# Placing each unit's value products directly ahead of the next unit's scores, and moving a tile's first unit, in a fused attention and two-layer feed-forward kernel

## The chip, the cores and the metric

The kernel runs on one core of a Trainium2 chip. The metric is the device time of one execution in microseconds (us); the time before is the median of three runs. One further execution was taken by the hardware profiler, and all rows below come from it.

## What is computed

Chunked attention with a few memory keys, then two feed-forward blocks. All in float32.

```python
# q, k, v: (4, 8, 768, 64); mem_k, mem_v: (4, 8, 8, 64)
for c in range(24):                                  # chunks of 32 positions
    q_c = q[:, :, 32*c : 32*c + 32]
    ctx = slice(max(0, 32*c - 16), min(768, 32*c + 40))
    k_full = concatenate([mem_k, k[:, :, ctx]], axis=2)
    v_full = concatenate([mem_v, v[:, :, ctx]], axis=2)
    out[chunk] = softmax(q_c @ k_full.T / 8) @ v_full
x  = out as (3072 tokens, 512)
h  = x @ w_in                                        # 512 -> 2048
x1 = softplus(h) @ w_out                             # 2048 -> 512
y  = ((x1 @ w_a) * (x1 @ w_b)) @ w_o2                # 512 -> 1536 -> 512
```

## The kernel before

The 3072 tokens are cut into 8 tiles of 384 (TT). For a tile, `emit_h` multiplies x by one block of 128 columns of w_in (12 products into one PSUM bank of tag "h", which has two banks), `emit_soft` makes softplus of it (three ScalarE activations that start from the bank, then a VectorE operation, line 558, that reads the bank for the last time, then a split into a high and a low part), and `emit_x1` multiplies by w_out two rounds later (LAG) into four "acc" banks. A tile has 16 such rounds f. Every product is done in three parts on split operands, which is why there are 12 matmuls where 4 would do. After the 8 tiles a last stage computes the second feed-forward block (lines 740 to 850); the change doesn't touch it.

The attention of tile t + 1 is computed between the products of tile t. Its work is cut into units of 128 queries of all 8 heads, three to a tile: units 3t + 3, 3t + 4 and 3t + 5 during tile t, called the first, middle and last unit of their tile here. In the code i is the unit's number less 3. Units 0 to 2 are computed ahead of everything, as blocks. Units 3 to 5 run during tile 0 with steps of their own (EARLY_STEPS). The steps of a unit are:

- load_v (SyncE): the values of the unit's two windows of 88 positions and the memory values, into the one set of value tiles vn (SETS = 1), which the products of the unit before must have read
- turn (VectorE): transposes of k and q into kt and qt (one buffer each), and two small ScalarE copies of the memory keys into kt
- scores (TensorE, line 430): 32 products of 64x64 weights with 96 columns into two banks of tag "att"
- soft, norm: softmax on VectorE, ScalarE and GpSimd
- flip, flip2 (VectorE): ten 32-row transposes of the weights into af (one buffer)
- values (TensorE, line 477): 32 products of 96x64 weights with 64 columns into one bank pxa of tag "att"; the first 16 use window 0 and the transposes of flip, the other 16 window 1 and those of flip2
- place: ScalarE and VectorE copy pxa into x of the next tile as a high and a low part (lines 484 and 485)

Where a step stands is fixed by hand. `plan` holds (time, unit, step); a time of 32t + s means slot s of tile t, and a slot is half a round: `att_at` is called after `emit_h` (even slots) and after `emit_x1` (odd slots) and issues all steps that are due. From the second tile to the last but one, TensorE, VectorE and SyncE execute in the order in which the program issues; ScalarE and GpSimd are ordered by the framework's scheduler.

`Loaded.fetch(t, part)` brings k and q of a whole tile into one buffer in four parts of eight DMAs (part 0 has up to four more for the edges of a sequence, and four on GpSimd's queue for the memory keys). It is issued during the tile before, after the turn of that tile's last unit, which must have read the buffer. The weights of the last stage are converted meanwhile by `Early` (fetch, top, value, store; five in a tile), whose DMAs are on the same SyncE queue.

The slots of a tile before, for units 9 and up: first unit: turn 30 and scores 32 counted from the tile before (thus 0 of the next), values 9, load of the next unit's values 10; middle unit: turn 9, scores 11, values 20, load 21; last unit: turn 19, fetch parts 20, 21, 22, 23, scores 21, values 30, load 31.

Of the kernel before, what the change touches and what calls it, by code (L numbers as in the profile page):

```python
# [9 lines left out]
F32 = mybir.dt.float32  # L10
# [12 lines left out]
         (3, "values"), (3.1, "place"))  # L23
START = 1.7
FIRST_STEPS = tuple((d + {"turn": 0.5, "flip": -1, "flip2": -1}.get(step, 0), step) for d, step in STEPS)
SETS = 1
EARLY_STEPS = (((4.9, "scores"), (5, "weigh"), (9, "flip_p"), (10.9, "values"), (11, "place")),
               ((12.9, "scores"), (13, "weigh"), (17, "flip_p"), (18.9, "values"), (19, "place")),
               ((21.9, "scores"), (22, "weigh"), (27, "flip_p"), (28.9, "values"), (29, "place")))
EARLY = len(EARLY_STEPS)  # L30
# [20 lines left out]
def attn_moe_moe2(ctx: ExitStack, tc: tile.TileContext, q, k, v, mem_k, mem_v,  # L51
# [7 lines left out]
    P = 128  # L59
# [6 lines left out]
    UPT = TT // QU  # L66
# [4 lines left out]
    KT = DM // P  # L71
# [6 lines left out]
        name=nc.get_next_instruction_name(), act_func_set_id=6, ins=[], outs=[]))  # L78
# [8 lines left out]
    ps = ctx.enter_context(tc.tile_pool(name="ps", bufs=2, space=PSUM))  # L87
# [18 lines left out]
    class Weight:  # L106


        def __init__(self, dst, key):
            self.dst, self.key = dst, key  # L110
# [114 lines left out]
    loaded = Loaded()  # L225
    vsets = [Values(i) for i in range(SETS)]

# [82 lines left out]
    class Block:  # L310
# [48 lines left out]
        def values(self):  # L359
            self.px = px = self.psum(4, "pxb")[:, :KT * QB].rearrange("p (i t) -> p i t", i=KT)  # L360
            for i in range(KT):
                for j in range(2):
                    r = slice(64 * j, 64 * j + 64)
                    nc.tensor.matmul(px[r, i], lhsT=self.vn[:, 2 * i + j, :], rhs=self.af[:, i, r], start=True, stop=True)
# [28 lines left out]
    class Unit:  # L393


        def __init__(self, u):
            self.u = u
            self.b, self.n = divmod(u, NU)

        def load_v(self):  # L400
            self.v = vsets[self.u % SETS]
            self.v.fetch(self.b, self.n)
# [66 lines left out]
        def values(self):  # L469
            u = self.u  # L470
            vn = self.v.v
            self.px = px = ps.tile([P, 512], F32, tag="att", name=f"pxa{u}").rearrange("p (i t) -> p i t", i=KT)

            for w in range(2):
                for i in range(KT):
                    for j in range(2):
                        nc.tensor.matmul(px[64 * j:64 * j + 64, i, QB * w:QB * w + QB], lhsT=vn[:, w, 2 * i + j],  # L477
                                         rhs=af[:, 2 * w:2 * w + 2, KT * j + i], start=True, stop=True)
# [18 lines left out]
    blocks = [Block(u) for u in range(BPT)]  # L497
    units = [Unit(u) for u in range(B * NU)]

    plan = []  # L500
    for i, unit in enumerate(units[UPT:]):
        at = 2 * NF1 * (i + 1) // UPT - START + NEXT_LATER * (i == EARLY) - (i % UPT == UPT - 1)
        steps = FIRST_STEPS if i % UPT == 0 else STEPS
        if i < EARLY:
            steps = EARLY_STEPS[i]
            at = steps[-1][0]
        plan += [(at + d - steps[-1][0], i, getattr(unit, step)) for d, step in steps]
        if i < SETS:
            plan.append((2 + i, -1, unit.load_v))
        if i + SETS < len(units[UPT:]):  # L510
            plan.append((at + 1, i, units[UPT + i + SETS].load_v))
        if i % UPT == UPT - 1 and unit.u + 1 < len(units):
            turned = at + steps[0][0] - steps[-1][0]
            plan += [(turned + 1 + part, i, partial(loaded.fetch, unit.u // UPT + 1, part)) for part in range(KT)]
    plan += [(at, -1, lambda i=i: packed[1].turn(i)) for i, at in enumerate(PACKED_AT)]
    plan.sort(key=lambda p: p[:2])
    plan.reverse()
# [546 lines left out]
```

## Time and profile before

| | before |
|---|---|
| median of three runs | 1179.31 us (1178.32 to 1180.07) |
| the profiled execution | 1176.61 us, span 1174.8 us |
| TensorE busy | 1165.4 us, 99% of the span |
| VectorE, ScalarE, GpSimd busy | 62%, 45%, 23% |
| TensorE's granted clock | 1.00 of full speed (its upper level, 2.4 GHz) over the span |
| chain that ended last | TensorE 95%; pxa products 2%, sc products 1% |

Busy times are those of the profiled execution. TensorE's matmuls are pipelined: a row's length overlaps the next row's start, so the distance between starts tells what one costs. The chain that ended last follows the work back from the last instruction; in order of time it shows how long each group held up the end.

### The profile page before, as it was taken

Reading aid. Unit: us, or ns where it says so; the run is one execution under the profiler, and the core shown is the slowest. Engines: PE = TensorE matmul, PEld = TensorE weight load, DVE = VectorE, ACT = ScalarE, POOL = GpSimd, SP = SyncE. Lnnn points to the kernel's source line nnn. Section 1 sums busy time; section 2 is a strip of 40 time slices with the busy share of each in tenths; the row PEclk is TensorE's granted clock in tenths of the full one; section 3 lists DMA queues with packets and bytes.
Section 4 is the critical chain, followed back from the end, with each engine's and each line's share of the span. In section 5 each row is a group of like instructions: output and inputs, shape, how many; then the busy total and the mean of one; then the engine's idle time right before and its main releaser. Section 6 shows DMA issues by size and latency. Waiting matters only on the chain.

```text
span 1174.8 us, 20105 instructions
## 1 busy us (share of the span) xinstructions
PE 1165.4 (99%) x7462; PEld 1048.8 (89%) x7462; DVE 725.7 (62%) x1603; ACT 532.2 (45%) x1293; POOL 264.8 (23%) x239
## 2 busy tenths in 40 slices
PE   9899999999999999999999999999999999999998
PEld 6799999999999999999999888888888888888887
DVE  6888654556545665456377667867456657545555
ACT  6799666656566566665565332222211113111110
POOL 2000322323223222232233665721002101000000
PEclk9999999999999999999999999999999999999999
DMA  9965334353443534442374758464864443864301
GB/s 230 281 206 105 96 102 109 102 103 88 107 94 120 104 88 107 93 121 66 122 259 162 291 215 286 169 225 140 334 214 146 151 145 99 309 225 153 137 1 72
DMA packets 191154, 181.45 MB, mean 154 GB/s; under 512 B 120609, under 2 KB 149201, under 8 KB 191057
## 3 DMA queue, kind: packets, MB, share of 16 engines
q1 hardware_dynamic: 190672, 180.12, 49.2%
q8 instruction: 59, 0.97, 0.3%
q14 instruction: 39, 0.31, 0.1%
q0 software_dynamic: 384, 0.05, 0.0%
HBM read 129.79 MB, written 50.33 MB: 153 GB/s over the span
## 4 chain that ended last, share of the span: by engine, by line
PE 95%; DMA 2%; SPq 1%; ACT 0%; DVE 0%; issue 0%
PE px L571 23%; PE ph L547 22%; PE py L779 17%; PE pX L756 8%; PE pW L756 8%; PE pV L756 8%; PE pY L756 4%; PE pxa L477 2%; PE sc L430 1%; DMA kp<-in_k_dram 1%; DMA raw<-in_moe_w_in_dram 1%; SPq L331 1%; SPq L328 0%; PE sc L305 0%; PE pa L466 0%; SPq L102 0%
## 5 line engine op out<-in xcount | busy, mean ns | idle before, releaser
L547 PE MATMUL ph<-x,w 128*128 128x384 f32 x1536 | 289.7, 336 | 0.1
L571 PE MATMUL px<-gh,w 128*128 128x384 f32 x1024 | 283.2, 337 | 0.0
L547 PEld LDWEIGHTS ph<-x,w 128*128 128x128 f32 x1536 | 266.7, 188 | 2.2 <-issue 0.3
L779 PE MATMUL py<-w2o,c 128*128 128x512 f32 (+1 forms) x870 | 218.0, 388 | 0.0
L558 DVE SCALAR_TENSOR_TENSOR g<-ph,e 128x384 f32<-128x384 f32 x128 | 71.3, 557 | 206.3 <-ACT e L556 205.9
L779 PEld LDWEIGHTS py<-w2o,c 128*128 128x128 f32 x870 | 162.7, 188 | 33.5
L571 PEld LDWEIGHTS px<-gh,w 128*128 128x128 f32 x1024 | 186.7, 188 | 2.4 <-issue 0.2
L571 PE MATMUL px<-gl,w 128*128 128x384 f32 x512 | 171.2, 334 | 0.0
L838 ACT CAST c<-r 128x512 fp32r<-128x512 f32 x36 | 22.4, 621 | 308.2 <-DVE r L836 287.2
L538 POOL TENSOR_TENSOR gl<-g,gh 128x384 fp32r<-128x384 f32 x96 | 98.9, 1030 | 243.4 <-ACT gh L535 216.5
L554 ACT ACTIVATE e<-ph 128x384 f32<-128x384 f32 x128 | 62.2, 486 | 105.1 <-PE ph L547 91.0
L788 DVE TENSOR_TENSOR y<-py,y 128x512 f32<-128x512 f32 (+1 forms) x121 | 82.9, 685 | 36.2 <-PE py L779 36.0
L535 ACT CAST gh<-g 128x384 fp32r<-128x384 f32 x128 | 65.7, 513 | 73.8 <-DVE g L558 72.6
L571 PEld LDWEIGHTS px<-gl,w 128*128 128x128 f32 x512 | 96.1, 188 | 0.1
L448 DVE STREAM_TRANSPOSE af<-sm 32x256 f32<-32x256 f32 x180 | 78.2, 434 | 2.5
L555 ACT ACTIVATE e<-e 128x384 f32<-128x384 f32 x128 | 67.3, 526 | 4.0
L556 ACT ACTIVATE e<-e 128x384 f32<-128x384 f32 x128 | 67.3, 526 | 3.8
L835 DVE TENSOR_TENSOR d<-pW,q 128x512 f32<-128x512 f32 x36 | 24.9, 691 | 69.1 <-PE pW L756 69.1
L384 ACT ACTIVATE sm<-sm,st 128x96 f32<-128x96 f32 x168 | 60.5, 362 | 3.6 <-DVE st L380 3.6
L756 PE MATMUL pX<-x,u 128*128 128x512 f32 x216 | 54.8, 389 | 0.0
L756 PE MATMUL pW<-xs,u 128*128 128x512 f32 x216 | 54.8, 389 | 0.0
L756 PE MATMUL pY<-xs,u 128*128 128x512 f32 x216 | 54.8, 389 | 0.0
(162 smaller groups left out, 1636.7 us busy)
## 6 DMA issues: line engine op xcount, KB each, us to landing
u<-u_scratch SPq DMA_DIRECT2D x72, 512.0 KB
u_scratch<-u SPq DMA_DIRECT2D x36, 512.0 KB
w2o<-w2o_scratch SPq DMA_DIRECT2D x24, 512.0 KB
raw<-in_moe_w_in_dram SPq DMA_DIRECT2D x16, 512.0 KB
raw<-in_moe_w_out_dram SPq DMA_DIRECT2D x16, 512.0 KB
vn<-in_v_dram SPq DMA_DIRECT2D x35, 176.0 KB
raw_a<-in_moe_w_a_dram SPq DMA_DIRECT2D x12, 512.0 KB
raw_b<-in_moe_w_b_dram SPq DMA_DIRECT2D x12, 512.0 KB
```

What stands on the lines that cost most here:

```text
L448: nc.vector.transpose(out=af[32 * kb:32 * kb + 32, x], in_=self.sm[32 * x:32 * x + 32, :, 32 * kb:32 * kb + 32])
L535: anchor[0] = nc.scalar.copy(hi, val)
L538: engine.tensor_tensor(lo, val, hi.bitcast(F32), ALU.subtract)
L547: nc.tensor.matmul(ph, lhsT=w[:, a, kt * P:(kt + 1) * P], rhs=x[:, c, kt, :], start=n == 0, stop=n == 3 * KT - 1)
L554: nc.scalar.activation(e, ph, AF.Abs)
L555: nc.scalar.activation(e, e, AF.Exp, scale=-1.0)
L556: nc.scalar.activation(e, e, AF.Ln, bias=1.0)
L558: nc.vector.scalar_tensor_tensor(g, ph, 0.0, e, ALU.max, ALU.add)
L571: nc.tensor.matmul(acc[t][i][:, :TT], lhsT=a, rhs=c, start=f == 0 and m == 0, stop=f == NF1 - 1 and m == 2)
L756: nc.tensor.matmul(bank[:, :T2], lhsT=u[:, j, a, kt * P:kt * P + P], rhs=x[kt][:, c], start=first_ and m == 0, stop=m == 3 * KH - 1, skip_ ...
L779: nc.tensor.matmul(b, lhsT=c[:, x, r], rhs=w[:, y, cols], start=n == 0, stop=n == 3 * GROUP - 1)
L788: tt(y, b, y, ALU.add)
```

## The change

For 19 units the steps values and place are taken out of their own times and put 0.02 and 0.01 slots ahead of the scores of the next unit, in the same call of `att_at`. That holds for all units computed inside the tiles but unit 5 (the last of the first tile's three) and unit 23 (the last of all). Their pxa uses a bank of tag "h" in place of "att" (`own_bank`). For the first units 9, 12, 15, 18 and 21 (SOONER) turn moves 1.5 slots and scores, soft and norm 2.4 slots sooner. The load of the next unit's values moves from one slot after a unit's old time of placing to three, except behind a tile's last unit, where it stays. The four parts of the fetch move from 1, 2, 3 and 4 slots after the last unit's turn to 0.1, 0.9, 1.7 and 2.5.

The slots of a tile after, worked out from these numbers: turn of the next first unit 29; values of the last unit and scores of the next first unit 30; values of the first unit and scores of the middle one 11; values of the middle unit and scores of the last one 21; fetch parts 19, 20, 20, 21; an `Early` store 22; load of the last unit's values 23.

```diff
+SOONER = {"turn": -1.5, "scores": -2.4, "soft": -2.4, "norm": -2.4}
...
+            self.own_bank = False
...
-            self.px = px = ps.tile([P, 512], F32, tag="att", name=f"pxa{u}").rearrange("p (i t) -> p i t", i=KT)
+            self.px = px = ps.tile([P, 512], F32, tag="h" if self.own_bank else "att", name=f"pxa{u}").rearrange("p (i t) -> p i t", i=KT)
...
-    plan = []
+    plan, scored = [], {}
     for i, unit in enumerate(units[UPT:]):
         at = 2 * NF1 * (i + 1) // UPT - START + NEXT_LATER * (i == EARLY) - (i % UPT == UPT - 1)
...
-        plan += [(at + d - steps[-1][0], i, getattr(unit, step)) for d, step in steps]
+        sooner = SOONER if i % UPT == 0 and i > EARLY else {}
+        whens = [(at + d - steps[-1][0] + sooner.get(step, 0), step) for d, step in steps]
+        scored[i] = dict((step, a) for a, step in whens)["scores"]
+        if i % UPT and i > 0 or sooner:
+            plan += [(scored[i] + d, i - 1, getattr(units[UPT + i - 1], step)) for d, step in ((-0.02, "values"), (-0.01, "place"))]
+            units[UPT + i - 1].own_bank = True
+        plan += [(a, i, getattr(unit, step)) for a, step in whens if step not in ("values", "place") or i % UPT == UPT - 1 and (i < EARLY or i == len(units) - UPT - 1)]
...
-            plan.append((at + 1, i, units[UPT + i + SETS].load_v))
+            plan.append((at + 1 if i % UPT == UPT - 1 else at + 3, i, units[UPT + i + SETS].load_v))
         if i % UPT == UPT - 1 and unit.u + 1 < len(units):
             turned = at + steps[0][0] - steps[-1][0]
-            plan += [(turned + 1 + part, i, partial(loaded.fetch, unit.u // UPT + 1, part)) for part in range(KT)]
+            plan += [(turned + 0.1 + 0.8 * part, i, partial(loaded.fetch, unit.u // UPT + 1, part)) for part in range(KT)]
```

## Rows read from the trace of the kernel before

**Rows 1.** The page, part 1: TensorE's busy time, share of the span, instructions.

```profile
PE 1165.4 (99%) x7462; PEld 1048.8 (89%) x7462; DVE 725.7 (62%) x1603; ACT 532.2 (45%) x1293; POOL 264.8 (23%) x239
```

**Rows 2.** Chain that ended last in order of time, 340 to 366: start, us, what.

```profile
342.64 2.08 PE px L571 x12
344.72 0.82 PE sc L430 x32
345.54 2.28 PE ph L547 x12
...
362.44 1.08 PE pxa L477 x32
363.52 2.28 PE ph L547 x12
```

**Rows 3.** The same chain, 310 to 322.

```profile
313.71 1.15 PE pxa L477 x32
...
317.18 1.01 PE sc L430 x32
```

**Rows 4.** TensorE timeline at three switches: start, us, line, operation, tiles, shapes, count.

```profile
362.10 0.34 PE L571 MATMUL px<-gh,w 128*128 128x384 f32 x1
362.37 0.28 PE L477 MATMUL pxa<-af,vn 96*64 96x64 f32 x2
...
16.88 0.27 PE L356 MATMUL pat<-ident,work 128*96 128x128 f32 x1
17.08 0.30 PE L305 MATMUL scb<-kt,qt 64*64 64x88 f32 x2
...
10.65 0.25 PE L288 MATMUL ptk<-ident,kp 100*64 100x100 f32 x1
10.70 0.86 PE L294 MATMUL ptq<-ident,qp 128*64 128x128 f32 x12
```

**Rows 5.** VectorE timeline at a tile's end, 335 to 342.

```profile
335.30 2.23 DVE L448 STREAM_TRANSPOSE af<-sm 32x256 f32<-32x256 f32 x5
338.87 0.56 DVE L558 SCALAR_TENSOR_TENSOR g<-ph,e 128x384 f32<-128x384 f32 x1 [1.33 <-ACT e L556]
...
339.94 0.70 DVE L411 STREAM_TRANSPOSE kt<-kn 128x512 f32<-128x512 f32 x1
...
340.89 0.67 DVE L414 STREAM_TRANSPOSE qt<-qn 128x512 f32<-128x512 f32 x1
```

**Rows 6.** TensorE timeline: values of a last unit at two tiles' ends.

```profile
263.17 1.22 PE L477 MATMUL pxa<-af,vn 96*64 96x64 f32 x32
...
337.06 1.22 PE L477 MATMUL pxa<-af,vn 96*64 96x64 f32 x32
```

**Rows 7.** Waits of SyncE's queue: who waited for whom, total us, times, longest.

```profile
SPq L188 <- DVE kt L413: 14.8, 5, 3.2
```

**Rows 8.** SyncE timeline of one fetch, 315 to 339.

```profile
315.23 0.33 SPq L188 DMA_DIRECT2D kn<-in_k_dram  x1
...
326.83 0.91 SPq L214 DMA_DIRECT2D vn<-in_v_dram  x2
327.83 0.77 SPq L673 DMA_DIRECT2D v_scratch<-val_o  x1
...
337.26 0.47 SPq L190 DMA_DIRECT2D qn<-in_q_dram  x1
337.82 0.91 SPq L214 DMA_DIRECT2D vn<-in_v_dram  x2
```

**Rows 9.** Stretches of half a microsecond: busy time by engine, PEclk, DMA share, GB/s.

```profile
338.50:339.00 0.50, 0.50 (x4) 0.50 (x4) 0.13 (x1) 0.50 (x2) 0.00 (x0) 1.00 0.60 101
...
339.50:340.00 0.50, 0.50 (x5) 0.50 (x4) 0.50 (x2) 0.47 (x1) 0.00 (x0) 1.00 0.86 196
```

**Rows 10.** SyncE timeline of another fetch, 241 to 263.

```profile
253.38 0.41 SPq L218 DMA_DIRECT2D vn<-in_v_dram  x1
...
262.00 0.47 SPq L190 DMA_DIRECT2D qn<-in_q_dram  x1
```

## The prediction

> **What bounds the kernel now.** I read the page first. TensorE is busy for 99% of the span [rows 1], so a change gains only by shortening what TensorE runs, and any wait put in front of TensorE is paid in full. The chain of waits in order of time then shows what the attention work costs between the big products. A group of twelve 128x384 products takes 2.08 us; a scores block takes 0.82 and the group behind it 2.28; a values block takes 1.08 and the group behind it 2.28 [rows 2]. So a unit pays 1.08 + 0.20 + 0.82 + 0.20 = 2.30 us. Two extras stand in the same view: a values block of a unit whose flips come late takes 1.15, and three scores blocks take 1.01 [rows 3].
>
> Where do the 0.20 and the start of a block come from? Starts in the TensorE timeline: the last big product starts at 362.10, the first values matmul at 362.37, 0.27 later where 0.17 is the pitch; the first pair inside runs late by about 0.05 more [rows 4]. So entering costs 0.15 and leaving 0.20: four switches a unit, 0.70 us.
>
> **The change, part by part.** The plan counts two slots a round of some 2.1 us each; slots are worked out from the plan's numbers (tile t starts at 32t).
>
> *Joining.* 19 units get their values directly ahead of the next unit's scores (all but the last of the first tile and the last of all). Leaving values (0.20) and entering scores (0.15) become one switch, from 96x64 to 64x64 tiles, that no row shows. Nearest rows: the transposes on 128 rows start last at 16.88 and the 64x64 scores behind them at 17.08, 0.20 later against a pitch of 0.11, plus 0.05 inside: 0.15. Lower bound: 100-row blocks passing to 128-row blocks of the same 64 columns start 0.05 apart, a switch for nothing [rows 4]. Upper bound: the two old switches, 0.35. I take 0.15, the row whose tiles change most alike: 0.20 x 19 = 3.8 us saved (6.7 to 0).
>
> *Bank and flips.* The values' result takes a bank of "h" in place of "att". Scores take both "att" banks, so the second of them waited for placing; I read the three blocks of 1.01 so, and that goes: 3 x 0.19 = 0.6. Six middle units run values one slot later, past the end of their flips, and should take 1.08 in place of 1.15: 6 x 0.07 = 0.4. The price: the next group needs the bank of the previous one, not of the one before. VectorE's read that frees it ends at 339.43 [rows 5], 2.4 us after its group ended at about 337.06 [rows 6]; the joined pair and a group of 2.08 stand in between, 4.2 us. Cost nothing, 1.8 us in hand. Placing and softmax now follow each other on VectorE (0.68 and some 1.5 us); behind them stands only the next such read. Cost nothing.
>
> *A tile's first unit.* In five tiles (first units 9, 12, 15, 18, 21) its transposes move from slot 30 to 29, ahead of the place step, and its scores from slot 32 to 30, straight behind the last unit's values. What is late next are the transposes. On VectorE the last flips end at 335.30 + 2.23 = 337.53, 0.47 after the values began at 337.06 [rows 5, 6]. Behind them the transposes of k and q take 339.94 to 340.89 + 0.67, 1.6 us [rows 5], so they would end 2.1 us after the values begin. The scores are due 1.1 after. That is a wait of 1.0 to 1.2 us with the handover, where before two slots covered it.
>
> *Its loads, and whom they pass.* SyncE issues in program order. The fetch is 32 DMAs, with 4 more for an edge, about 0.5 us each; the first waits for the transposes of the unit before, five times, 14.8 us in all [rows 7]. Asking a slot sooner therefore starts nothing sooner: it begins at 315.23 as before [rows 8]. What changes is the order. Before, the values' load of the tile's last unit stood between part 1 and part 2 (326.83, then a store at 327.83), ten microseconds ahead of its use. The plan now puts it at slot 23, behind all four parts (slots 19 to 21) and the store. The same issues in another order end at the same time, 337.26 + 0.47 = 337.73 [rows 8]; less the values' own 0.91 and its gap, and 0.4 that I guess of the store's 0.77 to have been a wait, their first issue is at 336.3.
>
> When do they land? Before, the next unit's values stood exactly there, behind the fetch: issued at 337.82 [rows 8], and the rate goes from the fetch's 101 GB/s to 196 by 339.5 [rows 9]. Their 2 x 88 rows x 2 KB = 360 KB take 1.8 us at 196 GB/s, so they are through by some 341.2: 3.4 us from issue to landing. Bounds: 2.3 if their bytes moved from the second issue on, 3.9 if the weights behind them slow them by half a microsecond. They land at 339.7. The values block would begin at 337.06 less 0.46 gained since the fetch (one join, one flip wait, one bank wait): 336.6, and needs the second load halfway through its 1.08, at 337.1. TensorE waits 2.6 us. By the end of the values the transposes are done, so the two waits don't add.
>
> Three tiles have this kind of edge, with the fetch still issuing when the values begin. In the other two (fetch ends 262.00 + 0.47 = 262.47, three value loads, the third 0.41 [rows 10], values at 263.17 [rows 6]): first issue 261.1, landing 264.5, needed 263.17 - 0.46 + 0.5 = 263.2: 1.3 us, about what the transposes hold too. Sum: 3 x 2.6 + 2 x 1.3 = 10.4 us. Bounds by the lag: 3 x 1.5 + 2 x 1.1 = 6.7 (the transposes hold the two) and 3 x 3.1 + 2 x 1.8 = 12.9.
>
> The Trainium skill has another price for the lag: "DMA: Bandwidth & Descriptors", Anatomy of one DMA, gives an estimate of a fixed 2.0 us plus bytes by 436 GB/s (it is fitted there on another issue path), 2.8 us for these loads. By it the waits would be 3 x 2.0 + 2 x 1.1 = 8.2 us and the sum 2.2 us smaller. The trace disagrees, with 3.4 us and 196 GB/s, and the sum goes by the trace.
>
> *Loads elsewhere.* The first tile puts its value load ahead of the fetch, as the plan sorts it, so nothing is late there. The load behind a first unit's values moves two slots, still nine ahead of its use; the one behind a last unit's stays. A few small mem_k DMAs on GpSimd move a slot with the fetch; nothing stands behind them. Cost nothing.
>
> *Sum.* Saved 3.8 + 0.6 + 0.4 = 4.8; waits 10.4; net +5.6 us. The profiled execution took 1176.61 us (span 1174.8, 1.8 around it), 2.7 under the median of 1179.31; the sum puts such an execution at 1182.2 and the median at **1184.9 us**.
>
> **Rivals.**
> *The values' load is in time* (not slower). Place: SyncE's queue ahead of the last unit's values. If the loads of the three tiles land 1.5 us sooner than I count, by lag or by quicker issues, only the transposes hold the scores: 5 x 1.2 = 6.0 against 4.8, +1.2, 1180.5 us, no change that can be told. For it: a store of 0.77 [rows 8] shows that the fetch's 22.5 us hold waits too. Against it: a load in just that place took 3.4 us.
> *Both waits are hidden*: the transposes too are done when the scores are due, so only the saving is left: 1174.5 us. That needs VectorE to end the flips 1.0 us sooner, and it began them right behind the read of its group. Little speaks for it.
> *The inner switch costs two old ones*: nothing is saved by joining, net +9.4, 1188.7 us. The Trainium skill ("TensorEngine Tiling (Array Packing)", Key Properties) says that a change of tiling mode drains TensorE; the page gives no time. It speaks against the free switch, to which I give no chance of its own. The 0.20 us between transposes and scores agrees [rows 4].
>
> **How the numbers follow.** Forecast 0.62; load in time 0.15; nothing saved 0.11; both hidden 0.12. A measurement of this kernel tells about 0.2%, 2.4 us, from no change: faster is below 1176.9, slower above 1181.7. The forecast with its bounds (waits 6.7 to 12.9, saving 1.0 to 7.7) could reach 1178.3 to 1191.2, both ends only if all errs one way; for 8 in 10 I take **1179 to 1189.5**, which holds the load-in-time and nothing-saved cases and leaves the hidden one out. Slower: most of the forecast (0.56) and nothing saved (0.11), 0.67. Same: load in time and the forecast's low end, 0.20. Faster: 0.13.
>
> **What would show it.** Right: a values block with the scores behind it at about 0.15 to 0.20 us from start to start, 2.1 us for the pair; TensorE idle in five places only, ahead of or inside the values of units 8, 11, 14, 17 and 20, a tile's last, released by the load of vn on SyncE's queue, some 2 to 3 us each in three and 1 to 1.5 in two. SyncE's vn issue behind the last q issue. Wrong: no idle there (load in time), idle released by the transposes qt or kt alone, or a pair that takes 2.3 us. A wait of ph for its bank would mean that I mis-sized the cover.

## Result, and the profile after

The changed kernel took 1193.84 us in the median (1191.68 to 1196.94), the kernel before 1179.40 beside it: a ratio of 1.0121, 95% interval 1.010 to 1.0141. Forecast were 1184.9 us and a range of 1179.0 to 1189.5. The sign was right; 14.4 us slower is well past 5.6 and outside the range. The profiled execution, which all rows below show, is the slowest of the five, 3.1 us above the median.

The profiled execution of the changed kernel took 1196.94 us. Its page, parts 1 and 2 (the second row is the granted clock in 40 slices of 30 us):

```profile
PE 1169.7 (98%) x7462; PEld 1055.1 (88%) x7462; DVE 727.2 (61%) x1603; ACT 534.0 (45%) x1293; POOL 263.6 (22%) x239
PEclk9999998999989999999999999999999999999999
```

TensorE has the same 7462 instructions and is busy 4.3 us longer than in [rows 1] (less what the joins save), while the span grew by 20.4 us: most of the loss is idle time, and some is work that ran slower. Two slices fall below 0.9, where the kernel before had a mean of 1.00. Both parts are found at the places that the prediction names. The chain in order of time, at the end of the tile that holds the values of unit 11:

```profile
267.09 0.18 SPq L681
...
267.32 0.02 SPq L215
...
267.37 3.88 DMA vn<-in_v_dram
271.25 0.14 issue
271.38 1.98 PE pxa L479 x32
273.36 1.49 PE sc L432 x32
```

The chain has left TensorE and runs over a store and a load of SyncE's queue. The load takes 3.88 us to land, and the values that start behind it take 1.98 us where [rows 2] have 1.08. The waits of TensorE (who waited for whom, total us, times, longest):

```profile
PE pxa L479 <- DMA vn<-in_v_dram: 14.0, 6, 3.8
```

And SyncE's timeline there, which answers to [rows 8]: the last q, the store, then the values' loads, in the order forecast.

```profile
266.29 0.47 SPq L191 DMA_DIRECT2D qn<-in_q_dram  x1
266.86 0.41 SPq L681 DMA_DIRECT2D v_scratch<-val_a  x1
267.37 0.97 SPq L215 DMA_DIRECT2D vn<-in_v_dram  x2
```

The clock, in stretches (length, busy time by engine, PEclk, DMA share, GB/s): one ahead of the first such wait, then behind each of the five.

```profile
185.00:189.00 4.00, 4.00 (x25) 4.00 (x24) 2.72 (x7) 2.06 (x4) 1.12 (x2) 1.00 0.50 82
192.80:199.60 6.80, 6.63 (x75) 6.13 (x73) 2.20 (x17) 3.97 (x18) 1.00 (x1) 0.51 0.48 132
271.40:274.70 3.30, 3.30 (x64) 3.04 (x64) 0.93 (x2) 1.00 (x2) 1.00 (x3) 0.50 0.28 63
349.90:356.60 6.70, 6.62 (x75) 6.12 (x71) 2.20 (x17) 3.97 (x18) 1.00 (x1) 0.50 0.50 132
428.80:435.00 6.20, 6.20 (x88) 5.95 (x89) 2.56 (x19) 3.98 (x18) 1.01 (x1) 1.00 0.55 140
505.00:511.00 6.00, 5.91 (x86) 5.62 (x86) 2.32 (x18) 3.98 (x18) 1.02 (x1) 1.00 0.57 150
```

Behind three of the five waits TensorE ran at its lower level, 1.2 GHz. The gaps from the start of the last big product to the start of the values were 3.14, 2.79, 4.11, 2.53 and 2.94 us, where 0.27 is usual [rows 4]: 14.2 us more. In the three stretches it was busy for 6.63 + 3.30 + 6.62 = 16.6 us at half speed, which would cost some 8.3 us. Short waits are hidden in these busy times: inside four of the five values blocks the second half of the products starts 0.1 to 0.4 us later than usual (0.18 to 0.48 us behind the first half, where 0.05 is usual), about 1 us together.

Joined pairs look as forecast where they were made:

```profile
225.15 1.08 PE pxa L479 x32
226.23 0.82 PE sc L432 x32
227.05 2.31 PE ph L555 x12
```

By starts such a pair costs 2.106 us and the two blocks apart 1.284 + 1.024, so it is 0.20 shorter. But among units 15 to 23 six pairs stand apart as before (values, a group of big products, then scores), where the section on the change says that all 19 are joined:

```profile
382.08 1.15 PE L479 MATMUL pxa<-af,vn 96*64 96x64 f32 x32
385.45 0.89 PE L432 MATMUL sc<-kt,qt 64*64 64x96 f32 x32
```

The reason is in the plan's arithmetic: the scores' time is computed as 139.00000000000003, which `att_at` issues in slot 140, and 0.02 less falls in slot 139. Six of the 19 joins were never made.

### The profile page after: what moved, and what is told of

The parts are those of the page before. It is cut to its first block, busy times and chain, and to the rows that moved or that the text cites. A ratio compares the mean times of both kernels' runs of the same rounds, so it can differ in the third digit from the quotient of the medians.

```text
span 1195.2 us, 20099 instructions
## 1 busy us (share of the span) xinstructions
PE 1169.7 (98%) x7462; PEld 1055.1 (88%) x7462; DVE 727.2 (61%) x1603; ACT 534.0 (45%) x1293; POOL 263.6 (22%) x239
## 4 chain that ended last, share of the span: by engine, by line
PE 82%; SPq 6%; DMA 4%; ACT 3%; DVE 3%; issue 1%; DVEq 0%
PE px L579 17%; PE ph L555 17%; PE py L787 16%; PE pX L764 8%; PE pW L764 8%; PE pV L764 8%; PE pY L764 4%; SPq L191 2%; SPq L189 2%; PE pxa L479 2%; DMA vn<-in_v_dram 2%; PE sc L432 1%; DMA kp<-in_k_dram 1%; SPq L332 1%; DMA raw<-in_moe_w_in_dram 1%
```

## Experiments

Start-up differs from execution to execution by some 7 us (unit 3's scores start at 52.1 to 58.8), so beside the ratios the table gives one stage, the same in all: from the start of the first scores product of unit 6 to the start of the first values product of the last unit, by the profiled execution of each. The mean clock is that of the whole span; in runs 1, 2, 4, 7 and 9 it holds a stretch at the lower level in start-up, at about 49 us, which the stage doesn't hold.

| kernel | ratio to before (95%) | mean clock | first, last start | stage, us | against before |
|---|---|---|---|---|---|
| before | | 1.000 | 125.12, 558.24 | 433.12 | |
| changed | 1.0121 (1.010 to 1.0141) | 0.993 | 126.20, 578.51 | 452.31 | +19.2 |
| 1 loads only | 1.0165 (1.0136 to 1.0194) | 0.991 | 130.33, 583.08 | 452.75 | +19.6 |
| 2 load put back | 1.0076 (1.0051 to 1.0101) | 0.994 | 128.12, 571.23 | 443.11 | +10.0 |
| 3 filled waits | 1.0106 (1.0088 to 1.0124) | 1.000 | 123.89, 568.24 | 444.35 | +11.2 |
| 4 joins alone | 0.997 (0.9957 to 0.9984) | 0.999 | 128.92, 558.66 | 429.73 | -3.4 |
| 5 turns 5 slots sooner | 1.046 (1.0439 to 1.0481) | 0.981 | 124.36, 611.81 | 487.45 | +54.3 |
| 6 joins, scores' bank | 1.0254 (1.0231 to 1.0277) | 0.991 | 124.46, 587.32 | 462.86 | +29.7 |
| 7 other queue | 1.0048 (1.0031 to 1.0065) | 0.999 | 127.97, 563.98 | 436.01 | +2.9 |
| 8 turns 2 slots sooner | 1.0033 (1.0017 to 1.0049) | 0.997 | 125.33, 563.60 | 438.27 | +5.2 |
| 9 changed, again | 1.0171 (1.0145 to 1.0197) | 0.991 | 128.44, 579.65 | 451.21 | +18.1 |

### 1. The change's loads alone

```diff
-            plan.append((at + 1, i, units[UPT + i + SETS].load_v))
+            plan.append((at + 1 if i % UPT == UPT - 1 else at + 3, i, units[UPT + i + SETS].load_v))
...
-            plan += [(turned + 1 + part, i, ...) for part in range(KT)]
+            plan += [(turned + 0.1 + 0.8 * part, i, ...) for part in range(KT)]
```

> The kernel before with the change's two edits of the loads alone: nothing is joined, nothing scored sooner. Theory A (the late value loads of the tiles' last units cost the time): the same five or six waits as in the changed kernel, 14 to 15 us together, and the half clock behind some of them, without the 3 to 4 us that the joins save: 1195 to 1201 us. Theory B (the transposes and scores that were moved ahead cost it, the loads are an accompaniment): 1179 to 1185 us. Theory C (the waits cost, the clock's fall belongs to the joined small products): about 1190 us at a mean granted clock of 1.00.

Measured: 1195.92 us, in the range of theory A. The values wait at the same five places, and the waits view has, as in the changed kernel,

```profile
PE pxa L477 <- DMA vn<-in_v_dram: 10.2, 6, 3.5
```

beside 2.4 us that it puts down to VectorE at one of the same places; by starts the five gaps are 12.4 us over the usual. The clock falls behind three of the five, with no joined pair in the kernel; behind the first:

```profile
198.80:205.50 6.70, 6.43 (x33) 6.34 (x34) 2.23 (x4) 1.33 (x4) 1.00 (x1) 0.50 0.46 132
```

So the two edits of the loads alone bring a loss as large as the whole change's. Theory A holds; theories B and C fall.

### 2. The load put back into the fetch

The load stands between the second and the third part of the fetch again; the last two parts follow it in the same slot.

```diff
+        if i % UPT == UPT - 1 and i > EARLY:
+            plan.append((scored[i] - 0.005, i - 1, unit.load_v))
...
+            plan += [(scored[i] - 0.004 + 0.001 * part if part > 1 and i > EARLY else turned + 0.1 + 0.8 * part, ...
```

> The changed kernel with only the value load of each tile's last unit put back into the middle of the fetch (behind its second part). Theory A: no wait for values is left, the clock stays at 1.00; the values then wait about 0.5 us for the second flips and the scores about 0.8 us for the transposes, 5 times, against 3.6 us saved by 13 joins and the freed banks: 1181 to 1184 us. Theory B (the sooner steps cost it): 1188 us or more.

Measured: 1185.42 us, between the ranges of the two theories. The wait for values is gone, but what stands next is larger than the 0.8 us expected:

```profile
PE sc L432 <- DVE qt L416: 8.7, 5, 2.7
```

VectorE's timeline shows two kinds of tile's end (idle time before and its releaser in brackets):

```profile
341.61 2.23 DVE L450 STREAM_TRANSPOSE af<-sm 32x256 f32<-32x256 f32 x5
345.15 0.71 DVE L413 STREAM_TRANSPOSE kt<-kn 128x512 f32<-128x512 f32 x1 [1.31 <-issue]
...
420.22 2.23 DVE L450 STREAM_TRANSPOSE af<-sm 32x256 f32<-32x256 f32 x5
422.72 0.67 DVE L413 STREAM_TRANSPOSE kt<-kn 128x512 f32<-128x512 f32 x1
```

At 420 the transposes follow the flips and the scores wait 1.33 us; at 341 VectorE idles 1.31 us first, probably because the loads put into the fetch push its end back (in the other tile of this kind the view names kn's DMA), and the scores wait 2.4 us. Behind the two long waits the clock fell too (0.51 from 346.2 to 353.0). So the clock's fall doesn't belong to the load, but to TensorE's standing still.

### 3. Work in place of the wait

```diff
+    def busy(t):
+        bank = ps.tile([P, 512], F32, tag="att", name=f"busy{t}")[:, :TT]
+        for n in range(14):
+            nc.tensor.matmul(bank, lhsT=w1[0][:, 0, :P], rhs=x_tile(t)[:, 0, 0, :], start=True, stop=True)
...
+            if sooner:
+                plan.append((scored[i] - 0.03, i - 1, partial(busy, unit.u // UPT - 2)))
```

> The changed kernel with 14 idle products of 128x384 (results unused) put ahead of the values of each tile's last unit, where TensorE would wait; by 0.165 us each they fill 2.3 us of a wait of 2.3 to 3.8 us. Theory A (TensorE's standing still lets the clock fall): the clock stays at 1.00 and 5 to 8.5 us come back: 1185 to 1189 us. Theory C (the clock falls for the small joined products, or for something else at that time): the clock falls again, 1193 us or more.

Measured: 1190.08 us, 1.1 above the range of theory A; the profiled execution has a clock of 1.000. In its stretches behind three of the waits:

```profile
191.00:198.00 7.00, 6.80 (x91) 6.50 (x92) 2.11 (x17) 3.79 (x18) 0.99 (x1) 1.00 0.46 131
267.00:271.00 4.00, 3.96 (x75) 3.67 (x76) 2.06 (x17) 2.15 (x8) 1.64 (x3) 1.00 0.42 91
342.60:349.00 6.40, 6.40 (x91) 6.21 (x91) 2.67 (x18) 4.08 (x18) 1.00 (x1) 1.00 0.55 138
```

The same late loads and the same joined pairs, at the upper level throughout: theory A, as far as the clock goes. The stage is 8.0 us shorter than in the changed kernel (452.31 to 444.35), though 70 products of 0.167 us, 11.7 us, and 2.4 us of waits that outlast them still stand there, together 14.1 us in place of the changed kernel's 14.2 us of waits ahead of the values. So 8.0 us is what the clock's falls cost there, with the 1 us of waits inside the blocks: 7 to 8 us for the clock. By whole times the gain is less sure: the ratio of 1.0106 is 1.8 us below the changed kernel's 1.0121, with overlapping intervals, and 7.7 below run 9's 1.0171; the stage compares the fastest execution of this run with the slowest of the changed kernel's five. Four of the six timed executions show a mean clock of 0.998 or 0.999; where in them the clock fell isn't kept.

### 4. The joins that need nothing sooner

```diff
+        if i % UPT and i > EARLY:
+            plan += [(scored[i], i - 1 + d, getattr(units[UPT + i - 1], step)) for d, step in ((0, "values"), (0.5, "place"))]
+            units[UPT + i - 1].own_bank = True
...
+        if i % UPT and i > EARLY:
+            plan.append((scored[i] + 0.05, i, unit.load_v))
```

> The kernel before with only the joins that need nothing sooner: values and placing of each tile's first and middle unit directly ahead of the next unit's scores, in one group and in a bank of the other tag; loads and fetch in the order of before. By the prediction's sums 12 joins at 0.20 us and some 0.5 to 1 us of waits for banks: 1175.5 to 1177.5 us. Rival (a joined pair gives back elsewhere what it saves, through the bank that the next product of the first layer needs or the values placed later): 1179 to 1181 us.

Measured: 1173.16 us, 0.3% faster than before and 2.3 us below the range given. All 12 pairs take 2.106 us (chain):

```profile
318.11 1.08 PE pxa L478 x32
319.19 0.82 PE sc L431 x32
320.01 2.31 PE ph L559 x12
```

The stage is 3.4 us shorter: 12 x 0.20 = 2.4, and the rest is as large as the waits for the bank and the flips that the prediction counted, 1.0. It is the fastest of all the kernels here.

### 5 and 8. The first unit's transposes out of the way

Run 5 moves the last unit's transposes, and so the fetch, 5 slots sooner, puts the next first unit's transposes ahead of the flips, the last unit's load behind the fetch that now ends sooner, and makes all joins in one group. Run 8 moves the last unit's transposes by 2 slots only and puts the first unit's between the two flips (-3.2 and 5.9 in place of the -5.5 and 2.2 below).

```diff
-SOONER = {"turn": -1.5, "scores": -2.4, "soft": -2.4, "norm": -2.4}
+SOONER = {"turn": -5.5, "scores": -2.4, "soft": -2.4, "norm": -2.4}
...
+        if i % UPT == UPT - 1 and i > EARLY:
+            whens[0] = (scored[i - 1] + 2.2, "turn")
...
+            plan += [(scored[i], i - 1 + d, getattr(units[UPT + i - 1], step)) for d, step in ((0, "values"), (0.5, "place"))]
...
+        if i % UPT == UPT - 1 and i > EARLY:
+            plan.append((scored[i] + 0.05, i, unit.load_v))
```

> The changed kernel with what its joins wait for moved out of the way: the last unit's transposes 5 slots sooner (right behind the middle unit's scores), so that the fetch starts 5 slots sooner; the first unit's transposes ahead of the flips instead of behind them; the last unit's value load behind the middle unit's values and the whole fetch; all joins made in one group (19). Theory A (the sooner scores cost nothing once transposes and loads are in time): no wait above 0.5 us at the tiles' ends, clock 1.00, 19 joins at 0.20 us and 0.9 us of small waits saved, some 0.7 us lost in the first tile: 1171 to 1173.5 us where the kernel before takes 1176.4. Theory B (the sooner steps hold up something else on VectorE or SyncE, whatever their place): 1176 us or more.

Measured: 1231.68 us, 4.6% slower. All joins are made, at 2.11 to 2.17 us without a wait, but TensorE stands for 8 to 11 us, five times, where a weight is converted:

```profile
267.91 0.43 DVE L682 TENSOR_SCALAR val_a<-raw_a 128x512 uint32<-128x512 uint32 x1 [14.77 <-DMA raw_a<-in_moe_w_a_dram]
```

```profile
269.96 3.93 PE L560 MATMUL ph<-x,w 128*128 128x384 f32 x12 [10.75 <-DVE x L487]
```

That weight's load is issued behind the fetch, which now runs ahead of it on SyncE:

```profile
263.12 0.47 SPq L191 DMA_DIRECT2D qn<-in_q_dram  x1
263.69 0.42 SPq L671 DMA_DIRECT2D raw_a<-in_moe_w_a_dram  x1
```

VectorE waits for it with the placing queued behind, and TensorE's next group waits for x. That is theory B, by way of SyncE's order. That it would be so whatever the place isn't shown: in run 8 these stalls are gone.

> As the run with the sooner transposes, but the last unit's transposes and with them the fetch only 2 slots sooner than in the changed kernel, behind the last weight load of the tile on SyncE, and the first unit's transposes between the two flips. If the stalls of that run came from a weight load behind the fetch: they are gone, the 19 joins stay at 2.11 us without a wait, 1171 to 1174 us where the kernel before takes 1177. If the transposes ahead of the second flips hold VectorE up themselves: products wait for VectorE's g or the values for the flips, 1178 us or more.

Measured: 1181.09 us. The long stalls are gone, the joins are all made, and the wait has moved once more:

```profile
PE pxa L479 <- DVE af L450: 4.1, 4, 1.6
```

```profile
339.32 0.71 DVE L413 STREAM_TRANSPOSE kt<-kn 128x512 f32<-128x512 f32 x1 [2.04 <-DMA kn<-in_k_dram]
...
341.43 2.23 DVE L450 STREAM_TRANSPOSE af<-sm 32x256 f32<-32x256 f32 x5
```

The transposes ahead of the second flips wait for the fetch, and the flips, and with them the values, wait behind them. The second theory held, and behind the wait in one tile the clock fell (0.50 from 191.7 to 198.4). In neither of the two places tried were load, transposes and flips all through in time.

### 6. The joins in the scores' own banks

Run 4's kernel without its bank edit:

```diff
-            units[UPT + i - 1].own_bank = True
```

> The kernel with the 12 joins of first and middle units, but the values left in the scores' own bank tag, as before the change. If the bank edit matters: the second score bank is the one the values lie in, it waits for ScalarE's copy and VectorE's subtraction, 1.3 to 2 us 12 times: 1189 to 1198 us. If it doesn't (the placing is through in time): 1173 to 1177 us.

Measured: 1205.91 us, beyond the range given. The chain, at a joined pair:

```profile
144.28 1.11 PE pxa L478 x32
...
145.41 0.59 ACT x L485
...
146.02 0.70 DVE x L486
...
146.77 0.88 PE sc L431 x28
```

The scores' second bank waits for both halves of the placing, 19.5 us in 12 waits, and the mean clock is 0.991. So the change's one-word bank edit, which the prediction credits with 0.6 us, is what makes a join pay. The clock fell behind six of the 12 waits, three of 2.3 us and three of 1.6 (0.50 from 412.3 to 415.6, for one), and not behind three others of 1.6.

### 7. The last unit's load from another queue

```diff
+        if i % UPT == UPT - 1 and i > EARLY:
+            plan.append((scored[i] + 0.05, i, partial(unit.load_v, nc.gpsimd.dma_start)))
```

> The changed kernel with the value load of each tile's last unit issued from GpSimd's queue behind the middle unit's values, the fetch as in the changed kernel. If its place in SyncE's order made the load late: no wait for values, clock near 1.00; the scores still wait 0.8 to 1.5 us for the transposes, 5 times: 1178 to 1182 us. If the fetch's transfers under way made it late, wherever it is issued: value waits of 1 us or more stay, and the time stays at 1185 us or more.

Measured: 1183.00 us, 1.0 above the first range, clock 0.999. No wait for values is left; the scores wait for the transposes alone:

```profile
PE sc L431 <- DVE qt L415: 5.7, 5, 1.3
```

The fetch's transfers go on as in the changed kernel, so its place in SyncE's order made the load late. The stage is nearly accounted for: 5.7 of waits, less 11 joins of 0.20 and 0.9 of smaller waits, is +2.6; measured +2.9.

### 9. The changed kernel again

> The changed kernel once more, for the spread of its clock from run to run: 1.010 to 1.014 of the kernel before in all, each run slower by about as much as its mean clock lies lower. If the clock's fall were an accident of one profiled execution, some runs would show 1.00 and a time some 8 us lower.

Measured: 1198.06 us, a ratio of 1.0171 where at most 1.014 was expected, every run at a mean clock of 0.990 to 0.993. The five gaps were 3.87, 2.21, 3.60, 2.17 and 2.62 us, 13.1 over the usual, and the clock was at its lower level behind four of them. Which waits the fall follows changes from one execution to the next; that it follows some does not.

## Why the prediction was right or wrong

- **TensorE pays every wait in full**: right, and it undercounts. The forecast priced a wait at its length. The step that failed is the one that isn't in its sum: what TensorE does behind a wait. Of the stage's 19.2 us 7 to 8 (run 3 and the stretches) are products at 1.2 GHz behind waits, and no rival had it. The Trainium skill, "TensorE: Matmul & The Clock Gate" (HAM oscillation — how this bites in real kernels), describes this for a loop that waits so each time round: a wait for a transfer lets the engine fall back to half rate, and the work behind it starts there. The trace agrees behind three waits of five, and behind four of run 9's five.
- **The waits for the last units' values**: place, order on SyncE and releaser were right (run 7); the size was short, 14.2 and 13.1 us against 10.4, the upper end being 12.9. Two terms did it. The lag was 3.88 us from issue to landing (3.57 to 3.91 by the chain at the other four), against 3.4; and the credit for the second half of the values was wrong: the first products start only with the landing (271.25 landed, 271.38 started), and inside four of the blocks the second half waits 0.1 to 0.4 more. The two edges forecast at 1.3 us waited 2.5 and 2.3.
- **The price of a load**: the Trainium skill's "DMA: Bandwidth & Descriptors" (Anatomy of one DMA) gives an estimate of 2.8 us by its sum, as the forecast said. The trace disagrees further than the forecast's 3.4 did: 3.57 to 3.91.
- **The joins**: 0.20 us each was right to the hundredth (the scores start 0.152 us behind the last values product, where the prediction looked for 0.15 to 0.20), so both bounds of the inner switch are out. The count was wrong: 13, not 19, because the slots were read from the plan as exact decimals. That is 1.2 us. Two of the 13 lie in the first tile, where the stretch from unit 3's to unit 6's scores took 71.82 us for 71.62, so they brought nothing; 11 x 0.20 = 2.2 was saved, not 3.8.
- **Banks and flips**: 0.6 + 0.4 forecast; run 4's stage leaves 3.4 - 2.4 = 1.0. Right.
- **The cover of the new bank**: no wait of ph for its bank behind a joined pair; the one of 0.2 us (at 406.53) stands behind values that weren't joined. Right.
- **The transposes**: 1.0 to 1.2 us a switch if the load weren't there; run 7 has 5.7 / 5 = 1.1. Right. The forecast was also right that the two waits don't add.

Put together for the stage: 2.2 by joins and 0.9 by banks and flips saved, 14.2 waited, 8.0 by the clock and the waits inside the blocks: +19.1, measured +19.2. With the forecast's terms and these 8.0 alone it would have been 1192.9 us. That this lies so near the median of 1193.84 is partly luck: the waits, longer by 3.8 us, and the joins, short by 1.6, are those of an execution that is 3.1 us above the median.

The rival *load in time* is what run 7 made: forecast 1180.5 us, 1.2 over before, measured at 1.0048 of before, 5.6 us. The stage holds 2.9 of them; in the profiled execution its first start is 2.9 us later too (127.97 for 125.12), but that differs as much between executions of any of these kernels, so where the rest of the medians' difference lies isn't shown. *Both waits hidden* was forecast at 1174.5; neither run 5 nor run 8 could hide them with the sooner joins in.

What stays open: why of two waits of like length the clock fell behind one and not behind the other (2.79 and 2.94 us in the changed kernel, 1.6 and 1.6 in run 6).

## What to carry to other kernels

Ahead of an engine that is busy for 99% of the span, ask of each step that is moved what it must wait for in its new place, and then in which order the queue issues that: here a load moved by two slots came to stand behind the last 16 small DMAs of a fetch and a store, and with the clock it cost seven times what the joins saved (22.2 us against 3.1). Price a wait of TensorE with the slower products behind it, not by its length alone; take the part of a change that needs nothing sooner (the 12 inner joins, 0.3% faster) and leave the rest. Where a schedule is kept in floats, put two steps together by one key, not by a difference of 0.02, and give a result that is read between two uses of a bank a bank of its own.

## What was unexpected of the hardware

- TensorE's granted clock fell to 1.2 GHz behind single waits of 1.6 to 4 us between long stretches of full work (1.6 in run 6, 3.8 in the changed kernel), though not behind all of them, and the work behind them ran at that level for 3.3 to 6.8 us in the stretches shown. Filling the wait with idle products kept it at 2.4 GHz (run 3).
- Two loads issued one behind the other on SyncE (0.97 us for both) land close together: the products that need only the first load began 4.0 us after its issue (267.37 to 271.38), and those of the second waited for theirs 0.4 us at most at any of the five edges.
